# Attention scores of the three whole key tiles in 64x128 array tiles, two matmuls a term where four 64x64 ones stood

## The chip, the cores and the metric

The kernel runs on one core of a Trainium2 chip. The time is device microseconds from start to end of one execution; 481.54 us is the median of three runs of the kernel before (481.5 to 482.3). The trace of before is of one more execution, taken with the hardware profiler, whose own time was 484.39 us with a span of 482.6 us from the first to the last instruction.

## What is computed

Sigmoid attention over 4 batches, 12 heads, 448 tokens and a head width of 64, then a soft mixture of experts (8 experts of 4 slots), then a wide layer with a cosine gate. The change is in the first matrix product of the attention.

```python
S = q.shape[2]                                   # 448
scale = 1.0 / np.sqrt(q.shape[-1])               # head width 64
scores = scale * np.matmul(q, k.transpose(0, 1, 3, 2)) - np.log(S)
attn = 1.0 / (1.0 + np.exp(-scores))
attn_out = np.matmul(attn, v)
...
x = attn_out as (4 * 448, 768)
logits = x @ phi                                 # 32 slots; softmaxed over tokens and over slots
slot_out = relu((d.T @ x) @ w1) @ w2             # per expert
x = c @ slot_out
h = x @ w_in
out = (h * np.cos(h)) @ w_out
```

## The kernel before

The 48 pairs of batch and head are worked in 24 head pairs `i`: one head's q and k lie in partitions 0 to 63, the other's in 64 to 127. q and k are split into float16 high and low parts (`cast_upper`, `cast_lower` on VectorE, tiles `hi` and `lo`), so one score is the sum of three float16 products. Each head pair has four key tiles `g`: three of 128 keys and a last one of 64 keys.

`scores(i, g)` writes one PSUM pair of banks (`sc`, a ring of three): bank `j` is head `j`, partitions are keys, columns are the 448 queries. A matmul in it multiplies 64 rows (the head width) and is put on a quarter of the array: `quarters` lists (j, k), the head's row half `rows[j]` and the key half `rows[k]`. Four such matmuls, on the four quarters, make one term for 128 keys of two heads; three terms make a tile. The last tile (`g == 3`) uses the same four quarters for 64 keys by two halves of the queries.

`squash(i, g)` turns a PSUM pair into weights on ScalarE (Sigmoid, line 426). `attn_v(i, g)` multiplies them with v on TensorE in float32 (line 437): in two column halves of all 128 rows for the whole tiles, in the four quarters for the last tile (its weights are the tile `one`). The sums `av` are copied to tokens (line 447) and transposed (line 454) on VectorE.

The order of the work on every engine is set by a planner (`Plan`) from costs and ranks written by hand; costs are not touched by the change. For a head pair the order on TensorE is `scores` of tile 1, `attn_v` of tile 3 of the pair before, `scores` of tiles 2 and 3, `scores` of tile 0 of the next pair, then `attn_v` of tiles 0, 1, 2. In between, at the end of a batch, stand the router logits (`lg`), their copies (`w`) and the slot sums (`sl`, line 670). Loads of q and k (line 372), v (line 380) and of the expert weights (line 231) share SyncE's queue in one order, each waiting there for its buffer.

After the attention come the expert products (lines 1033 and 1067, with weights streamed from HBM) and the wide layer (lines 1308 and 1343).

Of the kernel before, what the change touches and what calls it, by code (L numbers as in the profile page):

```python
# [18 lines left out]
B, H, S, D = 4, 12, 448, 64  # L19
# [6 lines left out]
P = 128  # L26
# [142 lines left out]
def fused(ctx: ExitStack, tc: tile.TileContext, qk, vv, phi, w1, w2, w_in, w_out, out):  # L169
    nc = tc.nc  # L170
# [148 lines left out]
    with ExitStack() as at:  # L319
# [29 lines left out]
        sides = [slice(0, S // 2), slice(S // 2, S)]  # L349
        quarters = [(0, 0), (1, 1), (0, 1), (1, 0)]  # L350
# [57 lines left out]
        def scores(i, g):  # L408

            ps = ps_s.tile([P, 2, 512], F32, tag="sc", name=f"sc{i}_{g}")  # L410
            h, l = hi[i], lo[i]
            terms = [(h, h), (l, h), (h, l)]
            for n, (keys, q) in enumerate(terms):
                flags = dict(start=n == 0, stop=n == len(terms) - 1)
                for j, k in quarters:
                    at, to, first = rows[j], rows[k], S + g * P + (k * D if g < 3 else 0)
                    cols = slice(0, S) if g < 3 else sides[k]
                    nc.tensor.matmul(  # L418
                        ps[to, j, 0:cols.stop - cols.start], keys[at, first:first + D], q[at, cols], **flags
                    )  # L420
            aa[i, g] = ps

        def squash(i, g):
# [316 lines left out]
        def attention():  # L740
# [105 lines left out]
            def score(i, g):  # L846
                nonlocal chain
                chain = sc[i, g] = add(
                    "pe", (.56, .655, .56, .28)[g], lambda i=i, g=g: scores(i, g), [chain, lower.get((i, 0)), lower.get((i, 1))], ring="sc"
                )  # L850
# [167 lines left out]
    with ExitStack() as ex:  # L1018
# [3 lines left out]
        with tc.manual_schedule():  # L1022
# [66 lines left out]
            def choose(g, k):  # L1089

                ps = (e2[0, 1][:, 256:] if k else ps_so).rearrange("p (c m) -> p c m", m=P)
                for c in range(2 if k else 4):
                    nc.tensor.transpose(ps[:, c], sos[g, k][:, c * P:(c + 1) * P], ident)
                return ps
# [28 lines left out]
            for c in range(0, F // P - 2, 2):  # L1123
                w2_rows(1, c)
                if c == 0:
                    ps = [choose(0, k) for k in range(2)]
# [12 lines left out]
            ps = choose(1, 0)  # L1139
# [138 lines left out]
    first, second, whole_s = slice(0, S // 2), slice(S // 2, S), slice(0, S)  # L1278
# [368 lines left out]
```

## Time and profile before

| | before |
|---|---|
| median of three runs | 481.54 us |
| the profiled execution | 484.39 us, its span 482.6 us |
| TensorE (PE) busy | 461.4 us, 96% of the span |
| VectorE (DVE), ScalarE (ACT) busy | 340.0 us, 294.4 us |
| granted TensorE clock, mean | 0.995 |
| attention / experts / wide layer, roughly | 0 to 152 us / 152 to 240 us / 240 us to the end |

PE counts matmuls, PEld the loads of their stationary operand, which run beside matmuls. A matmul's time in the profile is from its start to its modelled end; matmuls overlap, so the rate is read from the distance of starts and not from durations. "Idle before, releaser" tells what ended an engine's idle time; "issue" means that the profile shows nothing that it waited for.

### The profile page before, as it was taken

To read this page: it belongs to the slowest core of one execution; us is meant where nothing else is said; L and a number is where in the kernel's file an instruction comes from. 1 tells how busy PE (TensorE), PEld (TensorE's weight loads), DVE (VectorE), ACT (ScalarE), POOL (GpSimd) and SP (SyncE) were. 2 spreads that over 40 slices of the span, in tenths; PEclk is the share of its full clock that TensorE was granted. 3 is DMA by queue.
4 is the path that set the end of the run, shared out by engine and by line. 5 is a ranking of instruction groups with operands and counts; after the bars stand their busy time and mean duration, and the time that the engine had idled before them with its cause. 6 is when DMAs were issued, how large, how long until landed. Compare 5 with 4: busy or idle time off the path is not lost.

```text
span 482.6 us, 11213 instructions
## 1 busy us (share of the span) xinstructions
PE 461.4 (96%) x4629; PEld 249.1 (52%) x4629; DVE 340.0 (70%) x710; ACT 294.4 (61%) x513; POOL 0.7 (0%) x7
## 2 busy tenths in 40 slices
PE   8999999999979999787999999999999999999996
PEld 6666666666546433232654545555555555555553
DVE  5789998778644244200799999989999985755853
ACT  5887867767635012000689898678689866466550
POOL 0000000000000000000000000000000000000000
PEclk9999999999989999999999999999999999999999
DMA  8999888987938999999957430340220030200303
GB/s 257 343 395 368 291 249 299 353 264 251 300 100 293 355 414 415 414 416 384 415 204 246 149 133 1 97 166 0 89 87 1 1 115 0 82 34 1 114 2 114
DMA packets 33555, 99.13 MB, mean 205 GB/s; under 512 B 3808, under 2 KB 18400, under 8 KB 32736
## 3 DMA queue, kind: packets, MB, share of 16 engines
q1 hardware_dynamic: 33360, 98.30, 56.4%
q8 instruction: 36, 0.59, 0.5%
q14 instruction: 15, 0.12, 0.1%
q10 hardware_dynamic: 144, 0.11, 0.1%
HBM read 92.11 MB, written 5.51 MB: 202 GB/s over the span
## 4 chain that ended last, share of the span: by engine, by line
PE 73%; DMA 10%; DVE 9%; ACT 3%; issue 2%; SPq 2%; DVEq 0%; ACTq 0%
PE o L1343 40%; PE av L437 12%; PE sc L418 9%; DMA w<-in_w 6%; PE h L1033 4%; PE h L1308 2%; DMA wo<-in_w_out 2%; PE sl L670 2%; DVE wf L278 1%; ACT a L426 1%; DMA v<-in_vv 1%; DVE wo L281 1%; SPq L251 1%; DVE extra L1288 1%; SPq L985 1%
## 5 line engine op out<-in xcount | busy, mean ns | idle before, releaser
L1343 PE MATMUL o<-gh,wh 128*128 128x448 f16 (+1 forms) x361 | 127.6, 354 | 0.0
L1343 PE MATMUL o<-gl,wh 128*128 128x448 f16 (+1 forms) x361 | 127.0, 352 | 0.2 <-DVE gl L1321 0.2
L1343 PE MATMUL o<-gh,wl 128*128 128x448 f16 (+1 forms) x361 | 127.1, 352 | 0.0
L1343 PEld LDWEIGHTS <-wh 128*128 128x128 f16 x722 | 70.5, 98 | 71.9 <-issue 11.3
L426 ACT ACTIVATE a<-sc,bias_s 128x896 f32<-128x896 f32 x72 | 71.2, 1007 | 33.6 <-PE sc L418 25.0
L1288 DVE SCALAR_TENSOR_TENSOR extra<-extra 128x448 f32<-128x448 f32 x63 | 39.1, 621 | 16.7 <-ACT extra L1284 16.6
L1281 ACT ACTIVATE extra<-h 128x448 f32<-128x448 f32 x63 | 33.9, 538 | 26.2 <-PE h L1308 25.8
L1343 PEld LDWEIGHTS <-wl 128*128 128x128 f16 x361 | 35.4, 98 | 28.0 <-DVE wl L1186 0.3
L437 PE MATMUL av<-a,v 128*64 128x224 f32 x432 | 46.0, 358 | 3.7 <-issue 2.5
L1300 DVE SCALAR_TENSOR_TENSOR extra<-h,scales,extra 128x448 f32<-128x448 f32 x60 | 40.9, 681 | 8.1 <-ACT extra L1293 6.8
L1293 ACT ACTIVATE extra<-extra 128x448 f32<-128x448 f32 x63 | 36.1, 574 | 14.5 <-DVE extra L1288 14.2
L1321 DVE TENSOR_TENSOR gl<-extra,gh 128x448 f16<-128x448 f32 x60 | 37.2, 621 | 5.9 <-ACT gh L1317 5.7
L1317 ACT CAST gh<-extra 128x448 f16<-128x448 f32 x60 | 33.6, 559 | 12.3 <-DVE extra L1300 12.2
L418 PEld LDWEIGHTS <-hi 64*64 64x64 f16 x768 | 25.9, 110 | 23.5 <-issue 14.6
L1067 PE MATMUL so<-w,zone 128*32 128x512 f32 (+1 forms) x256 | 31.0, 490 | 7.3 <-DMA w<-in_w 7.3
L437 PEld LDWEIGHTS av<-a,v 128*64 128x64 f32 x432 | 29.1, 137 | 16.8 <-DVE xt L447 2.4
L1284 ACT ACTIVATE extra<-extra 128x448 f32<-128x448 f32 x63 | 36.4, 577 | 1.7
L418 PE MATMUL sc<-hi 64*64 64x448 f16 (+1 forms) x384 | 35.0, 352 | 0.9 <-ACT hi L404 0.4
L418 PE MATMUL sc<-hi,lo 64*64 64x448 f16 (+1 forms) x384 | 34.5, 341 | 0.0
L418 PE MATMUL sc<-lo,hi 64*64 64x448 f16 (+1 forms) x384 | 34.3, 339 | 0.0
L1308 PE MATMUL h<-ct,m 128*128 128x448 f32 x64 | 33.3, 521 | 0.7 <-DVE extra L1300 0.3
L447 DVE COPY xt<-av 128x448 f32<-128x448 f32 x24 | 14.9, 621 | 22.7 <-PE av L437 22.6
(192 smaller groups left out, 562.2 us busy)
## 6 DMA issues: line engine op xcount, KB each, us to landing
w<-in_w SPq DMA_DIRECT2D x28, 768.0 KB, 15.1
w<-in_w SPq DMA_DIRECT2D x38, 512.0 KB, 5.9
wo<-in_w_out SPq DMA_DIRECT2D x16, 768.0 KB, 5.5
raw<-in_qk SPq DMA_DIRECT2D x39, 224.0 KB, 4.5
w<-in_w SPq DMA_DIRECT2D x7, 1024.0 KB, 6.9
wi<-in_w_in SPq DMA_DIRECT2D x12, 512.0 KB, 8.0
late<-in_w_in SPq DMA_DIRECT2D x6, 1024.0 KB, 11.8
v<-in_vv SPq DMA_DIRECT2D x18, 224.0 KB, 5.1
```

What stands on the lines that cost most here:

```text
L418: nc.tensor.matmul(ps[to, j, 0:cols.stop - cols.start], keys[at, first:first + D], q[at, cols], **flags)
L426: nc.scalar.activation(a, ps, AF.Sigmoid, bias=bias_s, scale=qk_scale)
L437: nc.tensor.matmul(av[i][rows[j], k, 0:S // 2], v32[i][at, vc:vc + D], a[at, j, sides[k] if g < 3 else slice(0, S // 2)], start=g == 0, st ...
L1281: nc.scalar.activation(tmp[u][0][:, cols], hs[u][:, cols], AF.Copy, bias=0.25, scale=inv2pi)
L1284: nc.scalar.activation(tmp[u][1][:, cols], tmp[u][0][:, cols], AF.Copy, bias=magic)
L1288: nc.vector.scalar_tensor_tensor(out=ph[:, cols], in0=tn[:, cols], scalar=-magic, in1=ph[:, cols], op0=ALU.add, op1=ALU.subtract)
L1293: nc.scalar.activation(tmp[u][1][:, cols], tmp[u][0][:, cols], AF.Sin, scale=-2.0 * math.pi)
L1300: nc.vector.scalar_tensor_tensor(out=g[:, cols], in0=hs[u][:, cols], scalar=scale_of(u)[0], in1=tn[:, cols], op0=ALU.mult, op1=ALU.mult)
L1308: nc.tensor.matmul(h, m4[:, f * P:(f + 1) * P], ct4[:, t * S:(t + 1) * S], start=True, stop=True)
L1317: nc.scalar.copy(gs[u][1], gs[u][0])
L1321: nc.vector.tensor_sub(gs[u][2], gs[u][0], gs[u][1])
L1343: nc.tensor.matmul(ps, w[:, cols], g[:, at], start=begins(u) and n == 0, stop=ends(u) and n == len(terms) - 1 and at != first,)
```

## The change

In `scores`, the three whole key tiles are done with two matmuls a term in place of four: the stationary operand of a matmul is all 128 keys of a head (64 rows by 128 columns of the array), and the two heads lie in the two row halves. The last key tile keeps its four quarters. The results, their places in PSUM, and everything on the other engines are as before; the order of the groups of work on TensorE is the same, and the order of the instructions on VectorE, ScalarE, GpSimd and SyncE too.

```diff
             for n, (keys, q) in enumerate(terms):
                 flags = dict(start=n == 0, stop=n == len(terms) - 1)
-                for j, k in quarters:
-                    at, to, first = rows[j], rows[k], S + g * P + (k * D if g < 3 else 0)
-                    cols = slice(0, S) if g < 3 else sides[k]
-                    nc.tensor.matmul(
-                        ps[to, j, 0:cols.stop - cols.start], keys[at, first:first + D], q[at, cols], **flags
-                    )
+                first = S + g * P
+                for j, k in quarters if g == 3 else quarters[0:2]:
+                    at, to = rows[j], rows[k]
+                    if g < 3:
+                        nc.tensor.matmul(ps[:, j, 0:S], keys[at, first:first + P], q[at, 0:S], **flags)
+                    else:
+                        nc.tensor.matmul(ps[to, j, 0:S // 2], keys[at, first:first + D], q[at, sides[k]], **flags)
             aa[i, g] = ps
```

On TensorE, in the second head pair's work, the end of `scores` of tile 1 (`sc_1`), `attn_v` of the pair before's last tile (`av` from `one`) and the start of `scores` of tile 2 (`sc_2`) read so before (numbers behind names are buffers, the last figures are partitions by columns of the result):

```order
L418 LDWEIGHTS hi_126
L418 MATMUL sc_1_311<-lo_127,hi_126 64x448
L437 MATMUL av_284<-one,v_176 64x224 x4
L418 LDWEIGHTS hi_126
L418 MATMUL sc_2_332<-hi_126 64x448
```

and in the changed kernel so:

```order
L419 LDWEIGHTS hi_126
L419 MATMUL sc_1_287<-lo_127,hi_126 128x448
L438 MATMUL av_260<-one,v_176 64x224 x4
L419 LDWEIGHTS hi_126
L419 MATMUL sc_2_302<-hi_126 128x448
```

Nothing moved between the groups; the matmuls of line 437 (438 after), which still write 64 partitions, now stand between two groups that write 128.

A little later on TensorE, the end of `scores` of tile 2 and the start of the last tile's (`sc_3`) read before:

```order
L418 LDWEIGHTS hi_126
L418 MATMUL sc_2_332<-lo_127,hi_126 64x448
L418 LDWEIGHTS hi_126
L418 MATMUL sc_3_348<-hi_126 64x224
L418 LDWEIGHTS hi_126
```

and in the changed kernel:

```order
L419 LDWEIGHTS hi_126
L419 MATMUL sc_2_302<-lo_127,hi_126 128x448
L421 LDWEIGHTS hi_126
L421 MATMUL sc_3_312<-hi_126 64x224
L421 LDWEIGHTS hi_126
```

Here too the order is kept and only the result of tile 2 goes from 64 to 128 partitions; of the other kind of place, tile 3 to the next pair's tile 0, the same holds.

## Rows read from the trace of the kernel before

**Rows 1.** The page: span, busy time, share and instructions of engines; code queue.

```profile
span 482.6 us, 11213 instructions
...
PE 461.4 (96%) x4629; PEld 249.1 (52%) x4629; DVE 340.0 (70%) x710; ACT 294.4 (61%) x513; POOL 0.7 (0%) x7
...
q8 instruction: 36, 0.59, 0.5%
```

**Rows 2.** Busy time by stretch (us), clock, DMA share, GB/s.

```profile
24.00:150.00 126.00, 121.34 (x2221) 75.05 (x2214) 97.64 (x261) 90.77 (x145) 0.00 (x0) 0.99 0.83 286
150.00:240.00 90.00, 80.22 (x865) 35.80 (x861) 28.63 (x69) 14.74 (x32) 0.00 (x0) 1.00 1.01 396
```

**Rows 3.** Timeline of TensorE, one head pair: start, length, line, result<-operands, rows*columns, count.

```profile
63.83 1.11 PE L437 MATMUL av<-a,v 128*64 128x224 f32 x10
64.87 0.38 PE L418 MATMUL sc<-hi 64*64 64x448 f16 x4
65.09 0.36 PE L418 MATMUL sc<-hi,lo 64*64 64x448 f16 x4
65.28 0.36 PE L418 MATMUL sc<-lo,hi 64*64 64x448 f16 x4
65.46 0.55 PE L437 MATMUL av<-one,v 64*64 64x224 f32 x8
65.84 0.36 PE L418 MATMUL sc<-hi 64*64 64x448 f16 x4
...
66.41 0.27 PE L418 MATMUL sc<-hi 64*64 64x224 f16 x4
66.51 0.27 PE L418 MATMUL sc<-hi,lo 64*64 64x224 f16 x4
66.60 0.27 PE L418 MATMUL sc<-lo,hi 64*64 64x224 f16 x4
66.80 0.38 PE L418 MATMUL sc<-hi 64*64 64x448 f16 x4
...
67.18 0.39 PE L418 MATMUL sc<-lo,hi 64*64 64x448 f16 x4
67.50 0.60 PE L437 MATMUL av<-a,v 128*64 128x224 f32 x4
```

**Rows 4.** Instructions on av, 64 to 69 us: durations min/median/max in ns.

```profile
L437 PE MATMUL av<-a,v x26: 352/353/404, 63.8 to 68.9; 128*64 128x224 f32 x26
```

**Rows 5.** Timeline of TensorE, a change of columns alone, in the wide layer.

```profile
338.93 0.35 PE L1343 MATMUL o<-gh,wl 128*128 128x448 f16 x1
339.12 0.35 PE L1343 MATMUL o<-gl,wh 128*128 128x448 f16 x1
339.40 0.85 PE L1244 MATMUL late_m<-wi,s_acc 128*32 128x256 f32 x12
```

**Rows 6.** Timeline of TensorE, a 96-row and a 128-row shape.

```profile
151.98 1.02 PE L510 MATMUL lt<-lc,fold 96*128 96x224 f32 x4
152.87 1.02 PE L515 MATMUL lt<-xt,phi 128*128 128x224 f32 x4
```

**Rows 7.** Groups of weight loads: count, busy us, mean ns, idle before.

```profile
L1343 PEld LDWEIGHTS <-wh 128*128 128x128 f16 x722 | 70.5, 98 | 71.9 <-issue 11.3
L418 PEld LDWEIGHTS <-hi 64*64 64x64 f16 x768 | 25.9, 110 | 23.5 <-issue 14.6 <-DVE hi L396 0.2
```

**Rows 8.** Who waited for whom, to 150 us: in total, times, longest.

```profile
PE av L437 <- issue: 2.5, 1, 2.5
PE av L437 <- DVE xt L447: 1.2, 2, 0.7
...
PE lg L468 <- ACT a L426: 0.3, 1, 0.3
PE av L437 <- DVE hi L396: 0.2, 1, 0.2
```

**Rows 9.** The chain that ended last, 133 to 140 us: start, length, what.

```profile
133.08 2.13 PE sl L670 x98
135.20 1.66 PE av L437 x15
136.86 2.54 issue
139.40 0.53 PE av L437
```

**Rows 10.** Busy time by stretch around it, columns as in the second group.

```profile
135.00:140.00 5.00, 2.46 (x28) 1.20 (x24) 2.60 (x7) 0.00 (x0) 0.00 (x0) 0.94 0.05 16
140.00:145.00 5.00, 5.00 (x70) 2.86 (x68) 1.70 (x3) 2.66 (x4) 0.00 (x0) 0.72 0.40 119
```

**Rows 11.** SyncE's queue, 128 to 160 us: start, length, line, load, count.

```profile
128.86 1.75 SPq L231 DMA_DIRECT2D w<-in_w  x2
142.06 0.33 SPq L380 DMA_DIRECT2D v<-in_vv  x1
142.43 16.40 SPq L231 DMA_DIRECT2D w<-in_w  x6
```

## The prediction

> **What bounds the kernel now.** I read the page first: TensorE is busy 96% of the span [rows 1]. A share over the whole says little about one stage, so next come the stretches. From 24 to 150 us, the attention, TensorE is busy 121.34 of 126 us while VectorE has 97.64, ScalarE 90.77 and the DMA share is 0.83; from 150 to 240 us the DMA share is 1.01 [rows 2]. The change lies in the first of these, so the question is what TensorE's own time does there.
>
> Busy time can't answer it, since matmuls overlap; starts can. In the timeline of one head pair [rows 3] the reader is to see three distances. (1) Inside a group a round of four 64x64 matmuls over 448 columns follows the last one after 0.19 us (65.09, 65.28), and so it goes on into the float32 matmuls of line 437 on the same quarters (65.46) and back (65.84): 448 columns at the full 2.4 GHz are 0.187 us, so the array streams without a hole. (2) Where the shape of the array tile changes there is a hole. The ten rounds' tail at 63.83 ends at 64.94; one such matmul lasts 0.353 [rows 4], so the last started at 64.59, and the first of 64x64 starts at 64.87: 0.28 later, not 0.19. On the way back the last score starts at 67.22 (67.57 less 0.35) and the next 128x64 matmul at 67.50: again 0.28. So a change of shape costs 0.09 us. (3) After it the weights come late: the second round at 65.09 is 0.22 behind the first instead of 0.19 (0.03 lost), and the first float32 matmuls last 404 ns in place of 353 [rows 4], 0.05 lost.
>
> A wider view agrees that TensorE sets the pace: up to 150 us it waited 1.7 us in all for VectorE and ScalarE, and 2.5 us, once, for nothing that the profile shows [rows 8].
>
> **The change, part by part.**
>
> *The streaming.* A whole tile had 3 rounds of 4 matmuls, and gets 3 rounds of 2 with the same 448 columns. If two 64x128 matmuls run side by side as four 64x64 do, a round stays 0.187 us long. Rounds of two exist: the 128x64 ones go in steps of (1.11 - 0.353) / 4 = 0.19 us [rows 3], the same as rounds of four. So 432 matmuls and as many weight loads fewer (72 tiles x 6 each) are worth nothing here: 0. The Trainium skill has a rule that gives something else. TensorE: Matmul & The Clock Gate, "Measured speedup vs the span model", says that a pack of tiles takes one matmul's time and some 4 ns for each further tile; two tiles fewer in 216 rounds would save an estimated 1.7 us. Steps of 0.19 us for two tiles and for four speak against it; the sum goes by the rows.
>
> *The changes of shape.* This is the main term. Before, all the scores and the last tile's line 437 share one shape, so a head pair has two changes, into 128x64 and out of it. After it, 64x128 and 64x64 alternate: tile 1, the pair before's last tile, tile 2, tile 3, next tile 0 are five groups of alternating shapes, so a pair has six. Counted along TensorE's order up to the attention's end, with the logits, copies and slot sums in their places, 79 changes become 162: 83 more, of which 39 go into 64x128, 23 into line 437's quarters and 21 into the last score tile's quarters. No row shows this very pair of shapes. Nearest is a change in which only the columns differ, from 128x128 to 128x32: 339.12 to 339.40, 0.28 again where the step before is 0.19 [rows 5]. So I price each at 0.09 us: 83 x 0.09 = 7.5 us. Against that stands one place where a 96-row shape is followed by a 128-row one: four passes of 0.187 us take 0.89 us up to the next shape [rows 6], and the 0.14 us over must hold late weights as well; so perhaps not each change of figures is a change for the array. The bound from below is thus 0, kept as a rival. The Trainium skill, TensorEngine Tiling (Array Packing), "Key Properties", says that a change of the tiling mode, not of the tile within it, drains the engine; by it all 83 pay, and the sum is as it is here, while by the 96-row place alone there would be none of this term.
>
> *Late weights after a change.* 23 x 0.05 into float32 quarters and 21 x 0.03 into float16 quarters: 1.8 us. Into 64x128 the weights are 128 columns of float16. Loads of that width take 98 ns at 128 rows, less than the 110 of a 64x64 one [rows 7], so perhaps 0.02; twice the columns at the same rate would be 0.06. I take 0.03, as for the 64-wide, since the row of that width is not the longer one: 39 x 0.03 = 1.2 us (0.8 to 2.3). Where the old 23 changes out of 128x64 now go into 64x128, nothing changes at 0.03, up to 0.7 us more at 0.06. Together the new changes cost 7.5 + 1.8 + 1.2 = 10.5 us (9.9 to 12.3).
>
> *Waits that the lost time fills.* At 66.80 the next pair's tile 0 starts 0.20 us after the last quarter round where the step is 0.09 (66.51 to 66.60): it waits 0.1 us for a PSUM pair that ScalarE frees. Three changes more ahead of it use that up; ten such places give 1.0 us. The 1.7 us of waits for VectorE and ScalarE [rows 8] shrink likewise, but work that comes later on TensorE makes part of what they wait for later too; I take 1.2. That is -2.2 us (bounds -1.0 and -2.7).
>
> *The stall at 136.86 us.* After the slot sums TensorE stood still for 2.54 us [rows 9], for "issue", with the DMA share down to 0.05, since SyncE's queue was held at the load of line 380 until 142.06 [rows 10, 11]. Then the granted clock was low: means of 0.94 and 0.72 in two stretches of 5 us [rows 10] are 0.6 and 2.8 us at 1.2 GHz, half of which, 1.7 us, is lost. 36 transfers of the code queue carry 0.59 MB for 2 x 4629 instructions of TensorE [rows 1], about 257 each. The slot sums issue 112 matmuls, each with its weight load, in little more than 2.1 us [rows 9], so I read the stall as code that came late. The change takes out 864 instructions, and the border between two such pieces falls elsewhere. The most that it can give is 2.5 + 1.7 = 4.2 us; but three bursts of slot sums in the attention offer the same danger. The profiled execution is 2.85 us above the median, so the timed ones may hold little of this stall. I take -1.5 us (bounds -4.2 and, with a second stall, +2.0).
>
> *What it does behind the attention.* ScalarE, VectorE and DMA keep their order; each has slack against TensorE in the attention [rows 2]. From 150 us the DMA bounds. Does its work go on during a longer attention? Its queue was empty from 136 to 142 us, because the load at 142.06, and six weight loads behind it to 158.83, wait for buffers that the attention's last pairs hold [rows 11]. So the weights start later by what TensorE is late there, and the delay goes through whole.
>
> *The sum.* 10.5 - 2.2 - 1.5 = +6.8 us. On the profiled execution that is 484.39 + 6.8 = 491.2; if the stall went there entirely, 488.5. Against the median, 481.54 + 6.8, it is 488.3 us.
>
> **The rivals.** *No hole between 64x128 and 64x64* (both have 64 rows; rows 6 hint at it, rows 5 speak against it). Then only the stall's part is left: 481.54 - 1.5 = 480.0, or 477.3 with all of it. This is the other side; it decides when a change costs less than (2.2 + 1.5) / 83 = 0.045 us, half of each hole that the rows show. 8 in 100, since the one row for it stands against many holes. By the rule of the Trainium skill's TensorEngine Tiling (Array Packing) named above it would have no chance. *The two matmuls don't run side by side*: 72 x 3 more steps of 0.187 us, +40 us, 522 or more. The four quarters already run two row halves at once [rows 3], so 3 in 100. *More code stalls*: the bursts stay, the stall of 136.86 moves and does not go, and a second one comes: 488.3 + 1.5 + 2.0 = 491.8. 11 in 100. *The waits and the stall give back all that the changes cost*: at most 2.7 + 4.2 = 6.9 us against 9.9 at least; 2 in 100 for no change, if my counts are off.
>
> **How the numbers follow.** The forecast has 76 in 100. Its bounds are +9.9 - 2.7 - 4.2 = +3.0 and +12.3 - 1.0 + 2.0 = +13.3; 482.5 to 494.0 holds nearly all of it and the code stalls, and leaves out the first two rivals, 11 in 100, and the tails. A measurement here can tell about 0.2%, 1 us. Faster: the no-hole case nearly whole and a little of the tails, 0.08. Same: 0.05. Slower: 0.87.
>
> **What would show it.** In the timeline of a head pair each alternation of 64x128 and 64x64 has starts 0.28 us apart after a 448-column round (0.18 after a 224-column one), some 0.03 or 0.05 more in the next step, and rounds inside a group stay at 0.19. The weight loads of line 419 are half as many, 90 to 135 ns each. The wait at 66.80 is gone. The load that stood at 142.06 starts about as much later as the whole span is longer. I am wrong if the starts across such a border are 0.19 apart, or if rounds inside a group are 0.37 apart; and the size is off if idle for "issue" shows up after one of the slot sums.

## The result, and the profile after

The changed kernel takes 486.39 us (486.22 to 488.2, four runs) against 481.52 us (480.08 to 482.3, four runs of the kernel before): 4.9 us between the medians. The ratio on record is 1.0119, 95% interval 1.0098 to 1.014, which would be 5.7 us. A second, longer comparison (below, e7) gives 1.0114 (1.0085 to 1.0143), or 5.5 us, with 5.0 between the medians. So the change costs +4.9 to +5.7 us. Forecast were 488.3 us and +6.8, range 482.5 to 494.0.

The page of the kernel after, its first lines and the code queue, answers to [rows 1]:

```profile
span 484.4 us, 10349 instructions
...
PE 467.4 (96%) x4197; PEld 236.7 (49%) x4197; DVE 340.4 (70%) x710; ACT 295.5 (61%) x513; POOL 0.7 (0%) x7
...
q8 instruction: 33, 0.54, 0.4%
```

TensorE has 432 matmuls and 432 weight loads fewer and is busy for 6 us longer. The stretches of the kernel after, as in [rows 2]:

```profile
24.00:150.00 126.00, 124.71 (x1842) 64.16 (x1840) 97.00 (x258) 89.77 (x143) 0.00 (x0) 1.00 0.82 281
150.00:154.00 4.00, 4.00 (x38) 2.24 (x35) 1.15 (x5) 2.54 (x4) 0.00 (x0) 1.00 0.56 173
154.00:240.00 86.00, 76.71 (x812) 33.14 (x811) 26.56 (x65) 12.73 (x28) 0.00 (x0) 0.98 1.02 400
```

From 24 to 150 us TensorE is busy 124.71 us where it was 121.34, VectorE and ScalarE within 1 us of before, and the attention runs on past 152 us. The timeline of one head pair of the kernel after shows what fills TensorE; it answers to [rows 3]:

```profile
66.33 0.36 PE L419 MATMUL sc<-hi 64*128 64x448 f16 x2
66.53 0.35 PE L419 MATMUL sc<-hi,lo 64*128 64x448 f16 x2
66.72 0.35 PE L419 MATMUL sc<-lo,hi 64*128 64x448 f16 x2
67.00 0.61 PE L438 MATMUL av<-one,v 64*64 64x224 f32 x8
67.54 0.36 PE L419 MATMUL sc<-hi 64*128 64x448 f16 x2
67.74 0.35 PE L419 MATMUL sc<-hi,lo 64*128 64x448 f16 x2
67.93 0.35 PE L419 MATMUL sc<-lo,hi 64*128 64x448 f16 x2
68.21 0.29 PE L421 MATMUL sc<-hi 64*64 64x224 f16 x4
68.33 0.27 PE L421 MATMUL sc<-hi,lo 64*64 64x224 f16 x4
68.43 0.27 PE L421 MATMUL sc<-lo,hi 64*64 64x224 f16 x4
68.63 0.36 PE L419 MATMUL sc<-hi 64*128 64x448 f16 x2
68.83 0.35 PE L419 MATMUL sc<-hi,lo 64*128 64x448 f16 x2
69.02 0.35 PE L419 MATMUL sc<-lo,hi 64*128 64x448 f16 x2
69.30 0.98 PE L438 MATMUL av<-a,v 128*64 128x224 f32 x8
```

Read the starts. Inside a wide group a round of two follows after 0.19 to 0.20 us (67.74, 67.93), as a round of four did: no gain and no loss there. At each border between 64*128 and 64*64 the step is 0.28 (66.72 to 67.00, 67.93 to 68.21). Before, the way from the first round of tile 1 to the first of tile 2 took 0.97 us (64.87 to 65.84, [rows 3]); now it takes 1.21 (66.33 to 67.54).

But look at 68.43 to 68.63: 0.20 us for a 224-column round and a change of shape. In [rows 3] the same step, 66.60 to 66.80, took 0.20 with no change: it was then a wait for ScalarE. This change of shape cost nothing, since it took the place of a wait of the same length. Weight loads and matmuls of the wide line, instructions of line 419 of the kernel after (min/median/max in ns), below the weight loads of line 418 of the kernel before:

```profile
L418 PEld LDWEIGHTS <-hi x768: 102/107/174, 4.1 to 147.9; 64*64 64x64 f16 x192
L419 PEld LDWEIGHTS <-hi x288: 92/94/148, 4.1 to 148.9; 64*128 64x128 f16 x144
L419 PE MATMUL sc<-hi x144: 346/360/577, 4.5 to 148.7; 64*128 64x448 f16 x144
L419 PE MATMUL sc<-hi,lo x144: 347/349/577, 4.8 to 148.9; 64*128 64x448 f16 x144
```

The first matmul behind a change (sc<-hi) lasts 360 ns in the median, the others 349: late weights cost 0.01 us here, where I had taken 0.03. What TensorE waited for until 150 us in the kernel after, against [rows 8]:

```profile
PE sl L671 <- issue: 0.9, 1, 0.9
PE av L438 <- DVE xt L448: 0.4, 1, 0.4
PE sc L419 <- ACT hi L404: 0.3, 1, 0.3
```

The 2.5 us for "issue" behind the third slot sums are gone; 0.9 us stand in the second slot sums. The load of line 380 that started at 142.06 [rows 11] starts 1.4 us later, where the whole span is 1.8 us longer; SyncE's queue in the kernel after:

```profile
143.46 0.33 SPq L380 DMA_DIRECT2D v<-in_vv  x1
```

### The profile page after: what moved, and what is told of

The parts are those of the page before. It is cut to its first block, busy times and chain, and to the rows that moved or that the text cites. A ratio compares the mean times of both kernels' runs of the same rounds, so it can differ in the third digit from the quotient of the medians.

```text
span 484.4 us, 10349 instructions
## 1 busy us (share of the span) xinstructions
PE 467.4 (96%) x4197; PEld 236.7 (49%) x4197; DVE 340.4 (70%) x710; ACT 295.5 (61%) x513; POOL 0.7 (0%) x7
## 4 chain that ended last, share of the span: by engine, by line
PE 79%; DMA 10%; DVE 7%; issue 1%; ACT 1%; SPq 0%; DVEq 0%; ACTq 0%
PE o L1344 40%; PE av L438 14%; PE sc L419 10%; DMA w<-in_w 6%; PE h L1034 4%; DMA wo<-in_w_out 3%; PE h L1309 2%; PE sc L421 2%; PE sl L671 2%; PE so L1068 2%; DVE wf L278 1%; DVE wo L281 1%; PE lg L476 1%; DVE extra L1289 1%; PE late_m L1245 1%
## 5 line engine op out<-in xcount | busy, mean ns | idle before, releaser
L427 ACT ACTIVATE a<-sc,bias_s 128x896 f32<-128x896 f32 x72 | 72.5, 1007 | 36.3 <-PE sc L419 27.9
L419 PEld LDWEIGHTS <-hi 64*128 64x128 f16 x288 | 14.6, 95 | 26.6 <-issue 18.8
L419 PE MATMUL sc<-hi 64*128 64x448 f16 x144 | 26.8, 368 | 0.3 <-ACT hi L404 0.3
L1088 ACT COPY s_acc<-so 128x512 f32<-128x512 f32 (+1 forms) x3 | 1.4, 516 | 42.0 <-PE so L1068 42.0
L419 PE MATMUL sc<-lo,hi 64*128 64x448 f16 x144 | 26.2, 358 | 0.0
## 6 DMA issues: line engine op xcount, KB each, us to landing
late<-in_w_in SPq DMA_DIRECT2D x6, 1024.0 KB, 11.7
```

What stands on the lines that cost most here:

```text
L419: nc.tensor.matmul(ps[:, j, 0:S], keys[at, first:first + P], q[at, 0:S], **flags)
L427: nc.scalar.activation(a, ps, AF.Sigmoid, bias=bias_s, scale=qk_scale)
```

## The experiments

The theory was that of the holes: each change of array shape costs 0.09 us and some late weights, and no more. The rival: the wide tile itself costs, wherever it stands.

**One tile alone (e1, e2, e8).** Each kernel does one of the three tiles wide and the two others in quarters. The main line of the edit, against the kernel after; the lines left out put the quarters' matmul back for the other tiles:

```diff
-                for j, k in quarters if g == 3 else quarters[0:2]:
+                for j, k in quarters[0:2] if g == 0 else quarters:      # e1; g == 2 in e2, g == 1 in e8
...
```

> Only key tile 0 is done in 64x128, tiles 1 and 2 stay in 64x64 quarters. Theory of the holes (every change of array shape costs 0.09 us and some late weights): the attention has 99 changes of shape in place of 79, since tile 0 stands before line 437's matmuls, where a change was anyway; 20 x 0.105 = 2.1 us, of which about 1 us falls into the wait for ScalarE at that very place. Expected +1 us against the kernel before (+0.5 to +1.5). Rival (a wide tile itself costs, wherever it stands): a third of the 4.9 us of the whole change, +1.6 us, and the same for any of the three tiles.

> Only key tile 2 is done in 64x128; it stands between two groups in 64x64 quarters. Theory of the holes: 121 changes of shape in place of 79; 21 x (0.095 + 0.010) into it and 21 x (0.092 + 0.023) out of it are 4.6 us, less 1 to 2 us of waits that they fill. Expected +3 us (+2 to +4), two to three times tile 0 alone. Rival (a wide tile itself costs): the same as tile 0 alone, +1.6 us.

> Only key tile 1 is done in 64x128; a change out of line 437's 128x64 stands ahead of it anyway, the quarters of the last tile's line 437 behind it make one new change. Theory of the holes: 23 x (0.092 + 0.033) = 2.9 us, less 0.3 for shorter late weights at the old change and about 1 us of waits. Expected +1.5 us (+1 to +2.5); with tile 0 alone (+0.4) and tile 2 alone (+2.7) about the sum of the whole change. Rival (a wide tile itself costs): +1.6 us, but then also for tiles 0 and 2.

Measured against the kernel before: tile 0 1.0009 (0.9992 to 1.0026), +0.4 us; tile 2 1.0055 (1.0032 to 1.0078), +2.6 us; tile 1 1.0074 (1.0048 to 1.01), +3.6 us. The first two are near what the theory of the holes gave (e1 somewhat below its +0.5 to +1.5), the third is above its +1 to +2.5. Three groups with the same wide matmuls cost 0.4, 2.6 and 3.6 us, which speaks against a cost of the wide tile as such; what settles it are the starts, since rounds inside a wide group follow each other as the quarters do, in every one of these traces. The timeline of e1 at tile 0:

```profile
66.42 0.27 PE L422 MATMUL sc<-lo,hi 64*64 64x224 f16 x4
66.62 0.37 PE L419 MATMUL sc<-hi 64*128 64x448 f16 x2
66.82 0.36 PE L419 MATMUL sc<-hi,lo 64*128 64x448 f16 x2
67.01 0.36 PE L419 MATMUL sc<-lo,hi 64*128 64x448 f16 x2
67.30 2.49 PE L441 MATMUL av<-a,v 128*64 128x224 f32 x24
```

66.42 to 66.62 is the step of 0.20 us that the kernel before has too, and the change behind tile 0 was there before. In e8 the changes stand where TensorE waited for nothing; after the three dots come the end of tile 3 and the start of the next tile 0:

```profile
66.88 0.35 PE L419 MATMUL sc<-lo,hi 64*128 64x448 f16 x2
67.16 0.61 PE L441 MATMUL av<-one,v 64*64 64x224 f32 x8
67.59 0.37 PE L422 MATMUL sc<-hi 64*64 64x448 f16 x4
...
68.35 0.28 PE L422 MATMUL sc<-lo,hi 64*64 64x224 f16 x4
68.44 0.37 PE L422 MATMUL sc<-hi 64*64 64x448 f16 x4
```

0.28 to the quarters and 0.43 for their two rounds, 0.05 above two steps of 0.19; together 0.14 a pair, 3.2 us for 23 pairs. The wait at tile 0, at another place, is filled by it all the same: 68.35 to 68.44 is the bare step of 0.09 where [rows 3] has 0.20 (66.60 to 66.80), and over the whole attention that place gives back 1.7 us. So this one trace accounts for some 1.5 us, and its attention ends 1.2 us later than that of the kernel before in e6 (table below). The measured +3.6 is more than that, and the rest is open. The waits for "issue", which change from execution to execution (below), may have a part in it; until 165 us the traces of e1, e2 and e8 have, in this order:

```profile
PE av L441 <- issue: 0.2, 1, 0.2
PE av L441 <- issue: 3.0, 2, 1.8
PE av L441 <- issue: 2.1, 2, 1.4
```

That the three tiles add up to 6.6 us and not to the whole change's 4.9 to 5.7 lies within their intervals.

**The order (e3, e5).** In e3 the wide groups stand together and the quarter groups too; e5 is the kernel before with the same move.

```diff
-                score(i, 1)
-                sigma(i, 1)
+                for g in (1, 2):
+                    score(i, g)
+                    sigma(i, g)
                 if i:
                     value(i - 1, 3)
                 fill(2 * i)
-                for g in (2, 3):
-                    score(i, g)
-                    sigma(i, g)
+                score(i, 3)
+                sigma(i, 3)
```

> The changed kernel with one line of order moved: scores of tile 2 come ahead of the last tile's line 438 (line 437 before) of the pair before, so that wide groups stand together and quarter groups stand together. All wide tiles stay. Theory of the holes: 121 changes in place of 162; 41 x 0.115 = 4.7 us fewer than the changed kernel, if the order itself costs nothing, which the next kernel tells; expected 482 to 484 us. Against that next kernel it has 45 changes more, so about 45/83 of the changed kernel's loss, +2.7 us. Rival (a wide tile itself costs): no faster than the changed kernel; 4.9 us above the next one.

> The kernel before with the same move of order and no wide tile: the control of the order. 76 changes of shape in place of 79. Both theories: within 1 us of the kernel before unless the order itself makes ScalarE or VectorE late, which the sums of waits will show.

e3 missed its expectation, and e5 came out by the exception that its own names: e3 1.0244 (1.0212 to 1.0277), e5 1.0243 (1.0216 to 1.027), +11.7 us each. The order itself costs that much. The waits of weight loads until 150 us, in e5 and then in the kernel before, show where most of it lies:

```profile
PEld av L437 <- DVE xt L447: 9.3, 14, 3.1
PEld av L437 <- DVE xt L447: 2.4, 3, 1.2
```

These are 7 of the 11 us by which e5's attention ends later than e6's; the others were not taken apart. The last tile's matmuls of line 437 close a pair's sums in the one PSUM pair `av`; an order that has them 0.57 us later makes VectorE's copy of it (line 447) late for the next pair's line 437. So e3 can't tell the price of a change. It tells something else: 45 more changes of shape than in e5 cost nothing that these runs can tell (492.46 and 492.31 us) where TensorE waits this often for VectorE. The same waits could hide a cost of the wide tile, so the rival isn't refuted here.

**Fewer changes than before (e4).** Line 437's whole tiles in quarters too, each row half into a bank of its own. The kernel leaves out the addition of the two halves. Part of the edit, against the kernel before:

```diff
...
-                at = slice(0, P) if g < 3 else rows[k]
-                nc.tensor.matmul(
-                    av[i][rows[j], k, 0:S // 2], v32[i][at, vc:vc + D], a[at, j, sides[k] if g < 3 else slice(0, S // 2)],
-                    start=g == 0, stop=g == 3,
-                )
...
+                    vc, s = (3 * j + g) * D if g < 3 else VW - D * (j == r), k ^ r
+                    nc.tensor.matmul(
+                        av[i][rows[j], r, s * half:(s + 1) * half], v32[i][rows[r], vc:vc + D],
+                        a[rows[r], j, sides[k] if g < 3 else slice(0, half)],
+                        start=g == 0 and step == 0, stop=g == 3,
+                    )
```

> The kernel before, with line 437's matmuls of the whole tiles cut into quarters too, so that scores and line 437 share one array shape. It leaves out part of the computation: the two row halves are summed in different PSUM banks and one half of each sum isn't added, so that VectorE's work stays as it was. 32 changes of shape in the attention in place of 79; matmuls and weight loads on TensorE are 1152 instructions more, streaming is the same. Theory of the holes: 47 changes at 0.12 to 0.14 us are 5.9 us less on TensorE; some of it turns into waits for ScalarE and VectorE and into code waits, so 2 to 5 us faster than the kernel before. Rival (a hole only shows where the shape is new to the group, or instructions rather than holes cost): no gain, or slower by the added instructions.

Measured: 0.9992 (0.9965 to 1.0019), no gain, and below the expected 2 to 5 us. The holes did go. The timeline of e4 where scores turn into line 439 (line 437 before):

```profile
67.16 0.38 PE L418 MATMUL sc<-hi,lo 64*64 64x448 f16 x4
67.34 0.39 PE L418 MATMUL sc<-lo,hi 64*64 64x448 f16 x4
67.53 2.82 PE L439 MATMUL av<-a,v 64*64 64x224 f32 x45
```

0.19 from one to the other where before it was 0.28 (67.22 to 67.50, [rows 3]). Waits came in their place. The longest of TensorE in e4 until 165 us:

```profile
PE sl L673 <- issue: 1.9, 1, 1.9
PE av L439 <- DVE xt L450: 1.5, 1, 1.5
PE h L1036 <- issue: 1.4, 1, 1.4
PE sc L418 <- issue: 1.2, 2, 0.9
```

With 0.5 more at line 439 that is 5.0 us for "issue", in a kernel with 1152 instructions more on TensorE, where the trace of e6 below has 2.5. So some 3 of the 5.9 us expected from the holes came back as waits of these kinds. This one execution is still 1.9 us shorter than e6's (480.06 and 481.92 us), but the median of twelve is not, so the second half of the expectation, that the removed holes would show in the time, is not confirmed, and where the rest went is open.

**Both kernels once more (e6, e7).**

> The kernel before once more, for the stall of 2.54 us behind the third slot sums and the low clock after it. If it belongs to the program, it stands there again in this trace and in the timed runs; if it depends on when a code transfer gets through among the other transfers of that execution, it is gone, shorter or behind another slot sum, and the execution is up to 4 us shorter. Ratio to itself: 1.000 within 0.002.

> The changed kernel once more, for a tighter figure: +4.9 us by four runs. Sum from the two traces: 83 changes at 0.093 plus late weights make 9.1 us; waits that they fill 2 to 3.5. Expected +5 us (+4 to +7) over a before without its stall, and code waits, if any, behind slot sums.

e6 to the other runs of the kernel before: 1.0003 (0.9979 to 1.0028). e7 is the figure given at the start, +5.5 us, within its +4 to +7. In e6's trace the stall behind the third slot sums has shrunk to 0.4 us, and another stands in the first:

```profile
59.89 1.18 PE L670 MATMUL sl<-xT,ex 32*32 32x192 f32 x52
62.52 1.24 PE L670 MATMUL sl<-xT,ex 32*32 32x192 f32 x60 [1.45 <-issue]
...
68.44 0.38 PE L418 MATMUL sc<-lo,hi 64*64 64x448 f16 x4 [0.58 <-issue]
```

So it depends on the execution. Its time was 481.92 us, beside 484.39 of the first trace. The chains of waits of the ten traces have the first matmul behind the attention (`lt`) at these times:

| kernel | `lt` starts | span | from there to the end |
|---|---|---|---|
| before, first trace | 152.05 | 482.6 | 330.6 |
| before again (e6) | 149.83 | 480.1 | 330.3 |
| after | 153.67 | 484.4 | 330.7 |
| after again (e7) | 153.95 | 484.2 | 330.3 |
| tile 0 alone (e1) | 147.72 | 477.5 | 329.8 |
| tile 2 alone (e2) | 151.53 | 482.2 | 330.7 |
| tile 1 alone (e8) | 151.00 | 481.5 | 330.5 |
| order moved, wide tiles (e3) | 157.57 | 487.8 | 330.2 |
| order moved, no wide tile (e5) | 160.92 | 490.7 | 329.8 |
| line 437 in quarters (e4) | 147.40 | 478.3 | 330.9 |

What the attention loses or gains, the whole loses or gains: behind it everything keeps its length within 1.1 us. The two traces without the long stall, e6 and e7, differ by 4.1 us, near the 4.9 of the medians; both still hold shorter stalls, of which more below.

## Why the prediction held, point by point

*The streaming* is as said: steps of 0.19 us in rounds of two and four. The rule of 4 ns for each tile in a pack (the Trainium skill, TensorE: Matmul & The Clock Gate, "Measured speedup vs the span model") doesn't carry over to such a stream; no saving of 1.7 us is seen.

*The changes of shape* are as said: 0.28 in place of 0.19 at each border. The rival of no hole between 64x128 and 64x64 is refuted, and so is that of two matmuls one after the other. The Trainium skill's "Key Properties" of TensorEngine Tiling (Array Packing), that a change of mode drains the engine, agrees with these rows for a change of columns alone. What kept the rival alive, the 96-row place of [rows 6], is now clear from its single starts: the 0.14 us over are 0.10 of late weights at its first matmul and 0.03 at the change to 128 rows, so that change is not a full hole, but it isn't one of the 83 either.

*Late weights* are smaller into 64x128, 0.01 us for 0.03. Into the quarters of float32 they are the 0.05 that was taken: in the kernel after the first round there starts at 67.00 and the second, the line below, 0.24 later, where the step is 0.19.

```profile
67.24 0.37 PE L438 MATMUL av<-one,v 64*64 64x224 f32 x4
```

From first start to first start, between places without a wait, the medians of the two traces are (us):

| stretch of a head pair | before | after | longer by | places |
|---|---|---|---|---|
| tile 1 to line 437's quarters | 0.592 | 0.671 | 0.08 | 23 |
| these quarters to tile 2 | 0.378 | 0.542 | 0.16 | 20 |
| tile 2 to tile 3 | 0.568 | 0.672 | 0.10 | 21 |
| tile 3 to the next tile 0 | 0.285 | 0.414 | 0.13 | 19 |

With 0.2 us more where copies and logits follow, the 83 changes cost 10.0 us, where the forecast has 10.5. (Its lower bound of 9.9 should read 10.1 by its own terms.)

*The waits that the lost time fills* are a term that was mis-sized: 2.2 us, bounds 1.0 and 2.7. Comparing the first two traces place by place, the waits of TensorE that became shorter sum to 4.3 us: 2.2 at tile 0, more than half of it in ten places that lose 0.13 each (forecast 1.0); 1.6 before line 437 and the logits, at 20, 48, 120 and 130 us (forecast 1.2); and 0.5 behind four logits, which were left out. The list of waits has only the time in which no matmul is shown as running, and a matmul's shown end lies some 0.16 us behind the start of the next: shorter waits must be read from starts. Nor are the 1.7 us of [rows 8] all the waits for VectorE and ScalarE: the three dots there hide 1.1 and 0.4 us in the first 5 us.

*The stall* is the other term that was mis-sized. That it could vanish, shrink or move was right, and that the timed runs hold little of it too: e6 shows it in other places. In the first two traces it is worth far more than the -1.5 taken: 4.5 us in the kernel before (3.1 of standing still, 1.4 of slow rounds at the granted clock of 0.72) against 1.2 in the kernel after. Between e6 and e7, waits of this kind sum to 3.0 us (1.68, 0.75 and 0.59 above the normal step) and 1.5 us (0.93 and 0.57): -1.5.

*The start* is left out of this comparison, because it differs from execution to execution: rounds of 448 columns start 0.37 us apart at first, twice the later step, and the change to 0.19 comes at different times. The first matmul of line 437 starts at 9.93 us in the first trace of before and at 9.12 in e6, at 9.30 in that of after and at 9.51 in e7.

*Behind the attention* the delay goes through whole, as the table of `lt` shows. In sum: 10.0 - 4.3 = +5.7 us without the stall's part, 4.2 with -1.5; measured +4.9 to +5.7. So the runs leave little or nothing for the stall in the median, though at intervals of 1 us and more they can't exclude a part of it. The mechanism held, and the cost of the changes came within 5%; that the sum came out within 2 us is in part luck, since the waits were taken too small by 2.1 us and the stall, it seems, too large by up to 1.5.

## What to carry to other kernels

Count the changes of array shape along TensorE's order before choosing a shape for a group of matmuls: fewer and wider matmuls save nothing where rounds already stream at the clock, and a shape that its neighbours don't share cost 0.1 us a border here, and some late weights, wherever TensorE set the pace. Where TensorE waits anyway, at that border or behind it, the change is free up to the wait, as with tile 0; and taking changes out did not pay here, where it put 1152 more instructions into the stream. Take a control for a move of order: here the order alone cost 11.7 us, more than all the holes.

## What the hardware showed that I had not expected

Changes of shape cost the same, 0.09 to 0.10 us from step to step, for nearly all pairs of shapes in the attention of these traces (rows, columns or both); the exception is the one from 96x128 to 128x128, with 0.03 (single starts in the trace of before: 0.215 where the step is 0.189). The weights of 64x128 in float16 load in 94 ns, less than the 107 ns of a 64x64 quarter (medians).

The waits for "issue" are waits for code. Eight of the traces (all but e3 and e5) have 18 such waits of TensorE above 0.1 us until 165 us, of 0.1 to 2.5 us. Ahead of each, a transfer of the code queue ends 1.2 to 1.6 us before TensorE goes on (before: end at 137.94, on at 139.40; after: 100.26 and 101.70; e6: 61.13 and 62.52). The matmuls and weight loads of TensorE recorded ahead of the point where it goes on number 4801, 2753 and 1985 there; divided by 256, these leave 193, and so do all the 18, with no exception. A transfer holds 16 KB. So a kernel's order fixes the places where TensorE can run out of code, 256 of these records apart, and the execution decides at which it does: 4801 records in, the kernel before waited 2.5 us in its first trace and 0.4 in e6; 1985 in, 0.1 and 1.4. The Trainium skill, Runtime: NRT & Kernel Launch, "Instruction fetch mechanics", states blocks of 256 instructions and calls the cost of their borders mostly hidden. The first agrees with these counts, and so does the second at most borders, but not at these 18; the five longest waits stand in or just behind slot sums, whose 224 matmuls and weight loads use up most of a block within little over 2 us.
